# Two feed-forward matrix products as pairs of 64-partition matmuls in the column halves of the array

## The chip, the cores and the metric

The kernel runs on one core of a Trainium2 chip. The metric is the device time in microseconds of one execution, the median of several runs. A core has a matrix engine (TensorE, PE in the profile), a vector engine (VectorE, DVE), a scalar engine (ScalarE, ACT), a general engine (GpSimd, POOL) and an engine that issues transfers (SyncE, SP). Each of them works through its own instructions in the order of the program and waits for the others at semaphores.

## What is computed

Attention over 8 batches, 8 heads, 576 positions and 64 features, in which only the 32 largest scores of each row take part, and behind it a feed-forward block with the activation h·cos(h). All of it is in fp32.

```python
scores = scale * np.matmul(q, k.transpose(0, 1, 3, 2))          # scale = 1/8
kth = np.partition(scores, -top_k, axis=-1)[..., -top_k:-top_k + 1]   # top_k = 32
scores = np.where(scores >= kth, scores, -1000000000.0)
attn = np.exp(scores - np.max(scores, axis=-1, keepdims=True))
attn = attn / (np.sum(attn, axis=-1, keepdims=True) + 1e-09)
attn_out = np.matmul(attn, v)
x = attn_out.transpose(0, 2, 1, 3).reshape(4608, 512)            # (B*S, H*D)
h = x @ w_in                                                     # 512 -> 2048
g = h * np.cos(h)
out = g @ w_out                                                  # 2048 -> 512
```

## The kernel before

**Units and slots.** The 4608 token rows are cut into 36 blocks of 128. A unit is one block and one pair of heads, so there are 144 units, four to a block. The main loop (`slot`, L753) runs once for each unit. In a slot the program issues: VectorE's search for the 32 largest scores of unit i; ScalarE's mask and exponentials of unit i-1; the splitting of unit i-2 into half words by GpSimd and two transfers that bring it back transposed (`send`, L738); TensorE's scores of coming units; once in four slots P@V of four units (`values`, L456); and pieces of the feed-forward work of earlier blocks (`feed`, L671, by the table `plan`, L746). The order on each engine is fixed when the program is built; nothing is decided while it runs.

**Scores** (`scores`, L235). Contraction over 64 features, 64 query rows at a time: a matmul occupies 64 rows and 64 columns of the array, and the two heads and the two row halves of a unit take the four quarters. Each has 448 key columns, and a second group has the last 128 (into the bank called `rim`). A score buffer (`sc`, two of them) is free again when VectorE has read it at L267 (`fold_high`).

**P@V** (`values`, L456). The contraction runs over keys, in four chunks of 128 and one of 64 (`v_tail`, shared between heads). The output is transposed: 64 features of a head are the output partitions and 128 tokens the moving columns. The two heads of a pair go to the two column halves of the array, in alternating order: 128 rows by 64 columns for `v`, 64 by 64 for `v_tail`. The result lies in the free part of the `rim` banks. ScalarE's copy of the score ends (L257) reads the same banks, and VectorE multiplies by the reciprocal sums and writes `xT` (L491, L499).

**FF1** (`ff1`, L537). For a block, 16 slices f of 128 hidden features, each the sum over four chunks of 128 input features: the stationary operand is a 128 by 128 slice of `w_in`, the moving one is `xT`, 128 features by 128 tokens. One call makes two slices (8 matmuls), two calls fill one PSUM bank `mm` of 512 columns, so 16 matmuls are what stands together in the trace. ScalarE empties the bank twice (L567, L569 in `take_first`); GpSimd and ScalarE then make the cosine and the product g.

**FF2** (`ff2`, L618). For a block, 16 matmuls accumulate one 128 by 512 output `o`: the stationary operand is a 128 by 128 slice of g, the moving one 512 columns of `w_out`. One call makes two of the 16, two calls stand together. ScalarE scales the result into `ob` and sends it off (L638, L640). `mm` and `o` share two PSUM banks.

**Order on TensorE in the steady part.** One block, that is four slots: scores of two units, P@V of four units, FF2, FF1, FF2, FF1, scores of two units, FF2, FF1, FF2, FF1. After the last unit the program drains (`drain`, L823): two more P@V calls, each of two units, and the rest of the feed-forward work.

An fp32 matmul appears in the trace as two passes, each with a weight load (PEld) and a matmul row (PE). So the 2304 matmuls of FF1 are 4608 rows and the 576 of FF2 are 1152.

Of the kernel before, what the change touches and what calls it, by code (L numbers as in the profile page):

```python
# [17 lines left out]
P = 128  # L18
# [12 lines left out]
def kernel(  # L31
# [9 lines left out]
    nc = tc.nc  # L41
    ctx.enter_context(tc.manual_schedule())
    B, H, D, S = qT.shape
# [5 lines left out]
    NF = DF // P  # L49
# [29 lines left out]
    NC = DM // P  # L79
    FC = CW // P  # L80
    w_in = []
    w_out = []
    chunks = []
    for i in range(DF // CW):
        w = consts.tile([P, NC, CW], F32, tag=f"w_in{i}", name=f"w_in{i}")
# [4 lines left out]
    w = consts.tile([P, NF, DM], F32, tag="w_out", name="w_out")  # L90
# [421 lines left out]
    for w in widths:  # L512
        blk = {"t0": t0, "w": w, "left": 0, "g": [], "gated": []}
# [17 lines left out]
    def open_bank():  # L531

        if ff["open"] + len(full) == 2:
            take_banks()
        ff["open"] += 1

    def ff1(blk, i):  # L537
        w = blk["w"]
        nf = 256 // w
        part = i % 4  # L540
        if part == 0:
            blk["g"].append(ffw.tile([P, 1024], F32, tag="g", name="g", bufs=CHUNKS))
            blk["x"] = ffw.tile([P, 1024], F32, tag="x", name="x", bufs=XB)
            ff["live"] += 1
        if part % 2 == 0:
            open_bank()
            blk["mm"] = ps.tile([P, 512], F32, tag="mm", name="mm", bufs=2)
        g, mm = blk["g"][-1], blk["mm"]
        for a in range(nf):
            f = i * nf + a  # L550
            at = (part % 2 * nf + a) * w
            for c in range(NC):
                nc.tensor.matmul(  # L553
                    mm[:, at : at + w],
                    w_in[f // FC][:, c, (f % FC) * P : (f % FC + 1) * P],
                    blk["xT"][:, c],
                    start=c == 0,
                    stop=c == NC - 1,
                )
        if part % 2 == 0:  # L560
            return
        ff["open"] -= 1
        full.append((take_first, blk, g, blk["x"], mm, part // 2))
# [54 lines left out]
    def ff2(blk, i, f0):  # L618
        w = blk["w"]
        if f0 == 0:  # L620
            open_bank()
            blk["o"] = ps.tile([P, 512], F32, tag="mm", name="o2", bufs=2)
        o = blk["o"]
        per = 1024 // w
        for f in range(f0, f0 + 2):
            g = blk["g"][f // per]
            at = (f % per) * w + i * P
            nc.tensor.matmul(  # L628
                o, g[:, at : at + P], w_out[f], start=f == 0, stop=f == NF - 1
            )  # L630
        if f0 + 2 < NF:
            return
        ff["open"] -= 1
        full.append((take_second, blk, i, o))
# [27 lines left out]
    def item(kind):  # L662
        if not (can_first, can_second)[kind]():
            return False
        if kind == 0:
            ff1(*first.popleft())
        else:
            ff2(*second.popleft())
        return True
# [181 lines left out]
    for i in range(NU):  # L851
        ff["now"] += 1
        wq["ready"] = wq["done"]
        u, w, x = (units[i - n] if n <= i else None for n in range(3))
# [46 lines left out]
```

## Time and profile before

| | |
|---|---|
| median of 3 runs | 1413.0 us (1412.85 to 1414.05) |
| span of the profiled execution | 1410.6 us |
| TensorE busy | 1354.6 us (96%) |
| weight loads busy | 977.2 us (69%) |
| VectorE busy | 1336.9 us (95%) |
| GpSimd busy | 1165.3 us (83%) |
| ScalarE busy | 1140.9 us (81%) |
| granted clock of TensorE, mean | 0.975 |

The span goes from the first to the last instruction of one execution; the median of the runs is over whole executions. In the rows below, times are microseconds from the start of the span. A timeline row has start, length, engine, line and operation, the tiles written and read, the part of the array (rows*columns) for TensorE, the shape of the moving operand and the number of instructions merged (x32); what stands in brackets is how long the engine was idle before it and who ended that. The length of a merged row runs from the first start to the last end, and consecutive matmuls overlap in it, since the start of one does not wait for the end of the one before. The chain of waits follows the end of the execution back, at each step to what released it. The ends of matmuls are modelled in such a trace, so steps from start to start are used for TensorE.

### The profile page before, as it was taken

Reading aid. Unit: us, or ns where it says so; the run is one execution under the profiler, and the core shown is the slowest. Engines: PE = TensorE matmul, PEld = TensorE weight load, DVE = VectorE, ACT = ScalarE, POOL = GpSimd, SP = SyncE. Lnnn points to the kernel's source line nnn. Section 1 sums busy time; section 2 is a strip of 40 time slices with the busy share of each in tenths; the row PEclk is TensorE's granted clock in tenths of the full one; section 3 lists DMA queues with packets and bytes.
Section 4 is the critical chain, followed back from the end, with each engine's and each line's share of the span. In section 5 each row is a group of like instructions: output and inputs, shape, how many; then the busy total and the mean of one; then the engine's idle time right before and its main releaser. Section 6 shows DMA issues by size and latency. Waiting matters only on the chain.

```text
span 1410.6 us, 32284 instructions
## 1 busy us (share of the span) xinstructions
PE 1354.6 (96%) x11264; PEld 977.2 (69%) x11264; DVE 1336.9 (95%) x5004; ACT 1140.9 (81%) x2043; POOL 1165.3 (83%) x804
## 2 busy tenths in 40 slices
PE   5558999999999999999999999999999999999998
PEld 3445777777777777777777777777777777777775
DVE  7999999999999999999999999999999999999931
ACT  7887888888888888888888888888888888888831
POOL 4778988888888888888888888888888888898810
PEclk6788999999999999999999999999999999999999
DMA  9566776867675576668666576666766566655540
GB/s 291 193 196 181 204 178 169 203 172 196 162 177 152 161 199 159 181 160 197 174 170 159 152 181 187 170 170 160 207 165 165 158 174 166 148 157 146 152 101 15
DMA packets 427442, 240.12 MB, mean 170 GB/s; under 512 B 375952, under 2 KB 392592, under 8 KB 427280
## 3 DMA queue, kind: packets, MB, share of 16 engines
q1 hardware_dynamic: 420720, 224.22, 61.3%
q10 hardware_dynamic: 6560, 13.85, 2.8%
q8 instruction: 88, 1.44, 0.4%
q14 instruction: 74, 0.61, 0.1%
HBM read 45.09 MB, written 101.19 MB: 104 GB/s over the span
## 4 chain that ended last, share of the span: by engine, by line
PE 91%; DVE 7%; ACT 1%; DMA 0%; POOL 0%; issue 0%; SPq 0%; POOLq 0%
PE o L628 36%; PE mm L553 35%; PE rim L475 10%; PE sc L242 8%; DVE top L359 3%; PE rim L242 2%; DVE rest L364 2%; DVE low L364 1%; DVE rest L267 1%; DVE w_out L151 0%; DVE w_in L151 0%; DMA st<-in_moe_w_in_dram 0%; PE warm L844 0%; DVE low L275 0%; ACT s L387 0%; ACT s L378 0%
## 5 line engine op out<-in xcount | busy, mean ns | idle before, releaser
L553 PEld LDWEIGHTS mm<-xT,w_in 128*128 128x128 f32 x4608 | 537.9, 192 | 70.4 <-issue 65.5
L553 PE MATMUL mm<-xT,w_in 128*128 128x128 f32 x4608 | 539.2, 275 | 2.4 <-DVE xT L491 1.7
L628 PE MATMUL o<-w_out,g 128*128 128x512 f32 x1152 | 524.7, 599 | 0.0
L359 DVE MAX8 top<-rest 128x8 f32<-128x288 f32 x1152 | 479.0, 451 | 0.0
L364 DVE MATCH_REPLACE8 rest<-top,rest 128x288 f32<-128x288 f32 x864 | 376.7, 444 | 0.0
L628 PEld LDWEIGHTS o<-w_out,g 128*128 128x128 f32 x1152 | 207.7, 190 | 219.5 <-issue 214.8
L410 POOL COPY halves<-s 128x2304 uint16<-128x2304 uint16 x140 | 294.9, 2107 | 43.3 <-ACT s L387 40.1
L378 ACT ACTIVATE s<-s,top 128x576 f32<-128x576 f32 x288 | 207.6, 768 | 111.1 <-DVE top L352 99.0
L359 DVE MAX8 top<-low 128x8 f32<-128x288 f32 x576 | 241.8, 449 | 0.4 <-POOL low L292 0.4
L387 ACT ACTIVATE s<-s,nd 128x576 f32<-128x576 f32 x288 | 220.4, 769 | 1.1
L292 POOL TENSOR_TENSOR low<-low,rest 128x576 int32<-128x576 int32 x141 | 199.3, 1413 | 11.0
L283 POOL TENSOR_TENSOR low<-s 128x576 int32<-128x576 int32 x141 | 199.6, 1415 | 6.4 <-ACT s L259 6.4
L598 POOL TENSOR_TENSOR x<-g,x 128x1024 f32<-128x1024 f32 x68 | 161.2, 2370 | 5.7
L242 PE MATMUL sc<-k,q 64*64 64x448 f32 (+1 forms) x1120 | 145.6, 564 | 16.2 <-DVE low L275 9.8
L615 POOL TENSOR_TENSOR g<-g,x 128x1024 f32<-128x1024 f32 x68 | 161.0, 2367 | 0.0
L257 ACT COPY s<-rim 64x256 f32<-64x256 f32 (+1 forms) x280 | 103.1, 368 | 61.6 <-PE rim L475 60.0
L475 PE MATMUL rim<-ring,v 128*64 128x128 f32 (+1 forms) x2560 | 139.0, 268 | 0.0
L475 PEld LDWEIGHTS rim<-ring,v 128*64 128x64 f32 x2560 | 130.0, 139 | 6.5 <-issue 5.7
L253 ACT COPY s<-sc 128x896 f32<-128x896 f32 (+1 forms) x144 | 128.4, 892 | 3.3 <-PE sc L242 3.2
L567 ACT ACTIVATE g<-mm 128x512 f32<-128x512 f32 x144 | 85.2, 592 | 56.5 <-PE mm L553 55.5
L364 DVE MATCH_REPLACE8 low<-top,low 128x288 f32<-128x288 f32 x288 | 125.4, 443 | 0.0
L267 DVE TENSOR_TENSOR rest<-sc,s 128x576 f32<-128x576 f32 x144 | 107.7, 748 | 7.1 <-ACT s L259 6.6
(55 smaller groups left out, 1155.7 us busy)
## 6 DMA issues: line engine op xcount, KB each, us to landing
rows<-halves SPq DMA_DIRECT2D x140, 640.0 KB, 3.5
out_dram<-ob ACTq DMA_DIRECT2D x36, 256.0 KB, 2.1
q<-in_q_dram SPq DMA_DIRECT2D x31, 288.0 KB, 4.4
st<-in_moe_w_in_dram SPq DMA_DIRECT2D x16, 512.0 KB, 5.8
v<-in_v_dram SPq DMA_DIRECT2D x32, 256.0 KB, 4.2
k<-in_k_dram SPq DMA_DIRECT2D x31, 144.0 KB, 4.2
k<-in_k_dram SPq DMA_DIRECT2D x32, 128.0 KB, 4.5
st<-in_moe_w_out_dram SPq DMA_DIRECT2D x8, 512.0 KB, 5.1
```

Of the source, the lines that this page charges most:

```text
L242: nc.tensor.matmul(to[r0 : r0 + rows, rim_bank(r0, j) if k0 else place(u["hp"], j), 0 : k1 - k0], st["q"][d, q0 : q0 + rows], st["k"][d, k ...
L283: nc.gpsimd.tensor_tensor(out=u["low"].bitcast(I32), in0=s[:, :, 0:HS], in1=s[:, :, HS:S], op=ALU.add)
L292: nc.gpsimd.tensor_tensor(out=low, in0=low, in1=u["rest"][:, :, HS:S].bitcast(I32), op=ALU.subtract)
L359: nc.vector.max(to[:, j], src[:, j])
L364: nc.vector.match_replace(rest[:, j], to[:, j], src[:, j], NEG)
L378: nc.scalar.activation(out=s[:, j], in_=s[:, j], func=AF.Prelu, bias=less[:, j], scale=1.0, alpha=FAR)
L387: nc.scalar.activation(out=s[:, j], in_=s[:, j], func=AF.Exp, bias=nd[:, j : j + 1], scale=SCALE, accum_out=den[:, j, 0:1],)
L410: nc.gpsimd.tensor_copy(out=halves[:, :, 0 : 2 * S], in_=s.rearrange("p (k h) -> p h k", h=2))
L475: nc.tensor.matmul(to[d, r], lhsT, rhs, start=(bank, j) not in begun, stop=c == NT - 1 and u in us[-2:] and r0 + rows == P,)
L553: nc.tensor.matmul(mm[:, at : at + w], w_in[f // FC][:, c, (f % FC) * P : (f % FC + 1) * P], blk["xT"][:, c], start=c == 0, stop=c == NC - 1,)
L598: nc.gpsimd.tensor_tensor(out=x, in0=g, in1=x, op=ALU.subtract)
L628: nc.tensor.matmul(o, g[:, at : at + P], w_out[f], start=f == 0, stop=f == NF - 1)
```

## The change

Both products issue two matmuls where there was one. The stationary operand is cut into columns 0 to 63 and 64 to 127 (D is 64, P is 128), and the two outputs go to partitions 0 to 63 and 64 to 127 of the same PSUM region; the moving operand is the same for both. The two halves alternate within the accumulation. Nothing else is touched: the other engines' instructions, the order of the groups on TensorE and the waits between engines stand as before.

```diff
@@ ff1
             for c in range(NC):
-                nc.tensor.matmul(
-                    mm[:, at : at + w],
-                    w_in[f // FC][:, c, (f % FC) * P : (f % FC + 1) * P],
-                    blk["xT"][:, c],
-                    start=c == 0,
-                    stop=c == NC - 1,
-                )
+                for r0 in range(0, P, D):
+                    nc.tensor.matmul(
+                        mm[r0 : r0 + D, at : at + w],
+                        w_in[f // FC][:, c, (f % FC) * P + r0 : (f % FC) * P + r0 + D],
+                        blk["xT"][:, c],
+                        start=c == 0,
+                        stop=c == NC - 1,
+                    )
@@ ff2
             at = (f % per) * w + i * P
-            nc.tensor.matmul(
-                o, g[:, at : at + P], w_out[f], start=f == 0, stop=f == NF - 1
-            )
+            for r0 in range(0, P, D):
+                nc.tensor.matmul(
+                    o[r0 : r0 + D], g[:, at + r0 : at + r0 + D], w_out[f], start=f == 0, stop=f == NF - 1
+                )
```

## Prediction

> **What bounds the kernel now.** First the page: where the engines are full, and what the chain that ended last is made of.
>
> ```profile
> span 1410.6 us, 32284 instructions
> ...
> PE   5558999999999999999999999999999999999998
> ...
> DVE  7999999999999999999999999999999999999931
> ...
> PE 91%; DVE 7%; ACT 1%; DMA 0%; POOL 0%; issue 0%; SPq 0%; POOLq 0%
> ```
>
> TensorE and VectorE are both at nine tenths or more from the fourth slice to the last two, so the page alone does not say which of them sets the pace. The chain does: 91% of it is TensorE. I then looked at the chain inside the steady part, around one block of 128 tokens, which the program works on in four slots (columns: start, length, piece).
>
> ```profile
> 303.68 3.63 PE o L628 x8
> 307.31 3.57 PE mm L553 x32
> 310.88 3.44 PE o L628 x8
> 314.31 3.57 PE mm L553 x32
> ...
> 340.37 3.63 PE o L628 x8
> ```
>
> The piece at 303.68 comes back at 340.37: a block takes 36.69 us, and the chain through it is TensorE's work alone. An fp32 matmul is recorded as two passes, so x32 is 16 matmuls of FF1 (the first product, L553) and x8 is four of FF2 (the second, L628). Next, how much room VectorE has in the steady part, and what it waits for there.
>
> ```profile
> core 0: us, PE busy (x) PEld busy (x) DVE busy (x) ACT busy (x) POOL busy (x), PEclk, DMA share, GB/s
> 113.00:1340.00 1227.00, 1226.35 (x10466) 887.49 (x10460) 1215.45 (x4601) 1027.61 (x1833) 1080.60 (x736) 1.00 0.66 171
> ```
>
> ```profile
> DVE xT L491 <- ACT s L257: 7.1, 24, 0.8
> DVE xT L499 <- ACT s L257: 3.9, 7, 1.5
> ```
>
> In these 1227 us (33.4 blocks) TensorE is idle for 0.65 us and VectorE for 11.55 us, 0.35 us a block. Of that 11.0 us is one wait, that of the xT multiply for ScalarE's copy at L257. Two timeline rows of one block show who is late behind ScalarE:
>
> ```profile
> 303.72 0.74 ACT L257 COPY s<-rim 64x256 f32<-64x256 f32 x2 [1.64 <-PE rim L475]
> 304.50 0.49 DVE L499 TENSOR_TENSOR xT<-rim,ring 128x128 f32<-128x128 f32 x2 [0.30 <-ACT s L257]
> ```
>
> ScalarE stood 1.64 us until P@V (L475) was done with the PSUM banks they share, and VectorE stood 0.30 us behind it. So TensorE sets the pace and VectorE follows 1% behind it: **whatever TensorE saves beyond 0.35 us a block will not be seen in the time.** From here everything is worked out per block.
>
> **The change part by part.** It adds no arithmetic and no other engine's instruction: each matmul of 128 output partitions becomes two of 64, written to the two halves of the same PSUM region, in the alternating order of P@V. 5760 passes become 11520, and as many weight loads, each of 64 columns instead of 128.
>
> *FF1, 128 passes a block.* The shape after the change (128 rows, 64 columns, 128 moving) is that of P@V.
>
> ```profile
> 718.52 0.39 PE L553 MATMUL mm<-xT,w_in 128*128 128x128 f32 x2
> 721.87 0.28 PE L553 MATMUL mm<-xT,w_in 128*128 128x128 f32 x1
> 704.38 0.39 PE L475 MATMUL rim<-ring,v 128*64 128x128 f32 x4
> 707.66 0.28 PE L475 MATMUL rim<-ring,v 128*64 128x128 f32 x2
> ```
>
> The first pair of rows are the 2nd and the 32nd pass of one FF1 group: 30 steps in 3.35 us, 0.1117 us each. The second pair are the 2nd and the 32nd pair of passes of one P@V: 30 steps in 3.28 us, 0.1093 us for two halves together (x2 within 0.28 us, the length of one: they do run at once). The saving is 0.0023 us a pass, 0.30 us a block; two decimals of the rows leave it between 0.22 and 0.38.
>
> *FF2, 32 passes a block.* No row shows a half of 128 rows with 512 moving columns. The nearest are the scores, 64 rows and 448 columns.
>
> ```profile
> 708.40 0.59 PE L628 MATMUL o<-w_out,g 128*128 128x512 f32 x1
> 710.55 0.59 PE L628 MATMUL o<-w_out,g 128*128 128x512 f32 x1
> 703.08 0.56 PE L242 MATMUL sc<-k,q 64*64 64x448 f32 x4
> 703.46 0.29 PE L242 MATMUL rim<-k,q 64*64 64x128 f32 x4
> ```
>
> FF2 now steps 0.43 us (five steps from 708.40 to 710.55). Four score passes, two of them in either column half and with the same moving operand, start together and the next set follows 0.38 us later: 0.85 ns a column, against 0.84 for FF2. So a pair should also take 0.43 us, and I take no change. The bounds: the 0.0023 us that P@V gains over FF1 (a gain of 0.07 us a block), and 0.05 us a pass if a pair stalled as the first one of P@V does (next rows; a loss of 1.6 us a block). I stay at the near end because the P@V pairs and the 448-column sets both stream without such a stall.
>
> *Switches of the tiling mode, two a block, P@V to FF2 and scores to FF2.*
>
> ```profile
> 707.87 0.70 PE L628 MATMUL o<-w_out,g 128*128 128x512 f32 x1
> 723.96 0.29 PE L242 MATMUL rim<-k,q 64*64 64x128 f32 x4
> 724.18 0.70 PE L628 MATMUL o<-w_out,g 128*128 128x512 f32 x1
> 724.71 0.59 PE L628 MATMUL o<-w_out,g 128*128 128x512 f32 x1
> 704.00 0.29 PE L475 MATMUL rim<-ring,v_tail 64*64 64x128 f32 x4
> 704.22 0.33 PE L475 MATMUL rim<-ring,v 128*64 128x128 f32 x2
> ```
>
> After P@V's last pair (707.66) FF2 starts 0.21 us later and its second pass another 0.53 us later: 0.74. In one mode it would be 0.11 and 0.43: **0.20 us saved**. After the scores it is 0.22 and 0.53 (723.96, 724.18, 724.71); that switch stays, but into the mode of P@V, as from v_tail to v: 0.22 and then 0.16 instead of 0.11 for the first pair (704.00, 704.22, 704.38), 0.05 more than a step where FF2 now pays 0.10. **0.05 us saved.** From FF1 into the scores there is a switch before and after; no row shows it out of the column mode at this size, and I leave it as it is, with the 0.05 between the two kinds of first step as the bound on either side, twice a block.
>
> *Sum for TensorE:* 0.30 + 0.20 + 0.05 = 0.55 us a block, 18.4 us over 33.4 blocks, more than the 11.0 us that VectorE waits. So VectorE becomes the bound, if TensorE can get far enough ahead of it. The two nearest waits of TensorE in the block:
>
> ```profile
> 296.24 0.75 DVE L267 TENSOR_TENSOR rest<-sc,s 128x576 f32<-128x576 f32 x1
> 298.44 0.93 PE L242 MATMUL sc<-k,q 64*64 64x448 f32 x8
> 312.16 0.68 ACT L569 ACTIVATE x<-mm,quarter 128x512 int32<-128x512 f32 x1
> 314.15 1.05 PE L553 MATMUL mm<-xT,w_in 128*128 128x128 f32 x8
> ```
>
> The second score group needs the buffer that L267 reads: it starts 1.45 us after L267 ends. FF1 needs the bank that L569 empties: 1.31 us. So TensorE can lead by about 1.3 us more than now, and 0.30 to 0.8 us is enough for xT to find its operands ready. What is late next is then TensorE itself, behind VectorE at the scores, where it stands at no cost. **Steady part: 11.0 us** of the 11.55.
>
> *The end.* In the last two slices of the page VectorE has little left (3 and 1 tenths) and TensorE is full: there the time is TensorE's.
>
> ```profile
> 1342.40:1411.00 68.60, 26.14 (x224) 25.92 (x223) 0.99 0.19 55
> ```
>
> Seven FF1 groups, 224 passes by 0.0023, are 0.5 us, and the two P@V calls of the drain, each followed by FF2, are 0.4: **0.9 us**. And TensorE enters the end with the lead it has won, at most 1.3 us, of which I take **1.0**.
>
> *The instructions.* Twice as many FF1 and FF2 instructions have to be fetched, by a queue of their own:
>
> ```profile
> q8 instruction: 88, 1.44, 0.4%
> ```
>
> Even if all its 88 packets were doubled, that is 0.8% of the transfer engines' time. P@V already runs through two loads and two matmuls in 0.11 us, the rate that FF1 now gets, so I cost it at nothing; if a fetch came late, TensorE's lead of 1.3 us would cover it in the steady part, and it would show whole only in the end.
>
> *Sum:* 11.0 + 0.9 + 1.0 = 12.9 us off the span of 1410.6, 1397.7. The median of the runs, 1413.0, lies 2.4 us above this span, so the forecast is **1400 us**.
>
> **The rivals.**
>
> *A: FF2's pairs are a little dearer, and TensorE keeps the pace.* At 0.01 us a pass more, a block saves 0.55 - 0.32 = 0.23 us, 7.7 us over the steady part: 1405. For it: no row has such a pair at 512 columns. Against it: 0.85 and 0.84 ns a column.
>
> *B: slower. The next weight load is not hidden in FF2's pairs.* Place: every FF2 pass; price: the 0.05 us by which P@V's first pair, whose load nothing covers, exceeds a step. 1152 passes by 0.05 are 57.6 us, less 36 blocks by 0.55, 19.8: 1451. It decides from 0.017 us a pass on, where 32 passes eat the 0.55. For it: no row shows a load behind such a pair; against it: P@V hides the same loads beside passes a quarter as long.
>
> *C: it does not do what it is for, since VectorE is the bound already* and its 0.35 us a block is a fixed round trip. Then only the end is left: 1412. Against it: VectorE's wait stands behind P@V, which would come earlier.
>
> *D: VectorE does not bind* because its 99% has waits inside the records: all 36 blocks save 0.55 us, 1393. Against it: the two rows of waits account for 11.0 of its 11.55 idle.
>
> *E: no load is hidden between halves of the same rows.* Both products would then step as P@V's first pair does, 0.16 us: 4608 passes by 0.048 and 1152 by 0.05 are 279 us, less 0.25 by 36 for the switches: 1683. The P@V rows, 0.1093 us with 128 rows in both halves, speak against it. [...]
>
> **How the numbers follow.** The forecast gets 0.70, A 0.11, B 0.11, C 0.04, D 0.03, E 0.01. What a measurement here can tell from no change is about 0.2%, 2.8 us: faster are the forecast, A and D (0.84), the same is C (0.04), slower B and E (0.12). The range runs from 1396, which lets VectorE win its whole 11.55, the full lead of 1.3, 0.9 at the end and some 3 us of waits too short to show as idle, to 1409, which is A with half its saving left: it holds the forecast and A, 0.81.
>
> **What would show it.** In the profile after: FF1 groups of 64 passes in about 3.5 us with pairs 0.109 apart; FF2 pairs 0.43 apart; 0.11 between P@V's last pair and FF2; a block of 36.35 instead of 36.69 us; VectorE's waits at xT nearly gone and new waits of TensorE for VectorE (L267) or ScalarE, some 0.2 us a block; a chain with far more VectorE in it. The forecast is wrong if FF2 pairs step over 0.45 us, if pairs start one after the other, or if the xT wait stays while TensorE's blocks get shorter.

## The result, and the profile after

| | before | after |
|---|---|---|
| median of the runs | 1412.9 us | 1400.5 us |
| span of the profiled execution | 1410.6 us | 1397.0 us |

The ratio is 0.991, with a 95% interval of 0.9896 to 0.9924 (four runs of each; the 1413.0 us above are the median of three). The page of the changed kernel:

```profile
span 1397.0 us, 43804 instructions
## 1 busy us (share of the span) xinstructions
PE 1339.6 (96%) x17024; PEld 905.7 (65%) x17024; DVE 1334.2 (96%) x5004; ACT 1140.6 (82%) x2043; POOL 1169.3 (84%) x804
...
PE 59%; DVE 35%; ACT 2%; DMA 2%; POOL 1%; issue 1%; SPq 0%; DVEq 0%; POOLq 0%; ACTq 0%
```

TensorE and VectorE are busy for as large a share as before, so the busy shares tell nothing. The chain does: VectorE's part went from 7% to 35%, TensorE's from 91% to 59%. The windows view of the steady part (same columns as in the prediction) and VectorE's waits in it (who waits, for whom: us in total, times, longest):

```profile
113.00:1330.00 1217.00, 1214.45 (x15798) 821.79 (x15793) 1214.56 (x4606) 1028.78 (x1836) 1086.54 (x737) 1.00 0.66 174
```

```profile
DVE xT L499 <- ACT s L257: 1.2, 1, 1.2
DVE xT L491 <- ACT s L257: 0.7, 1, 0.7
DVE rest L267 <- ACT s L257: 0.6, 1, 0.6
```

VectorE was idle for 11.55 us in the 1227 us of the steady part and is now idle for 2.44 in 1217, in three waits. The 31 waits at xT have become two. Then TensorE's timeline, at the turn from P@V to FF2 and FF1 (L553 and L628 of before are L554 and L630 here):

```profile
337.59 0.39 PE L475 MATMUL rim<-ring,v 128*64 128x128 f32 x4
337.81 0.60 PE L630 MATMUL o<-w_out,g 128*64 128x512 f32 x2
339.96 1.03 PE L630 MATMUL o<-w_out,g 128*64 128x512 f32 x4
341.25 0.49 PE L554 MATMUL mm<-xT,w_in 128*64 128x128 f32 x5
344.52 0.39 PE L554 MATMUL mm<-xT,w_in 128*64 128x128 f32 x4
```

Two FF2 passes lie within 0.60 us, the length of one: the halves do run at once. Five pairs lie between 337.81 and 339.96, 0.43 us each, as full matmuls had taken. FF1's first and 31st pairs start at 341.25 and 344.52: 30 steps of 0.109 us. And FF2 starts 0.22 us after the last but one pair of P@V, that is 0.11 us after the last: the switch is gone.

What TensorE waits for now is what the prediction named, the score buffer that VectorE's L267 reads:

```profile
404.36 0.75 DVE L267 TENSOR_TENSOR rest<-sc,s 128x576 f32<-128x576 f32 x1
405.16 0.21 PEld L242 LDWEIGHTS sc<-k,q 64*64 64x64 f32 x8 [0.19 <-DVE rest L267]
405.16 0.61 PE L242 MATMUL sc<-k,q 64*64 64x448 f32 x4
```

The second score group starts 0.05 us after L267 ends, where it started 1.45 us after it before the change. It is so in 15 of the 32 blocks between 150 and 1280 us; in the others the distance is 0.2 to 0.9 us. Waits as short as this hardly show as idle time of TensorE, whose matmul ends are modelled.

### The profile page after: what moved, and what is told of

Same layout as the page of the kernel before. It is cut to its first block, busy times and chain, and to the rows that moved or that the text cites. A ratio compares the mean times of both kernels' runs of the same rounds, so it can differ in the third digit from the quotient of the medians.

```text
span 1397.0 us, 43804 instructions
## 1 busy us (share of the span) xinstructions
PE 1339.6 (96%) x17024; PEld 905.7 (65%) x17024; DVE 1334.2 (96%) x5004; ACT 1140.6 (82%) x2043; POOL 1169.3 (84%) x804
## 4 chain that ended last, share of the span: by engine, by line
PE 59%; DVE 35%; ACT 2%; DMA 2%; POOL 1%; issue 1%; SPq 0%; DVEq 0%; POOLq 0%; ACTq 0%
PE o L630 23%; PE mm L554 23%; DVE top L359 16%; DVE rest L364 10%; PE rim L475 7%; PE sc L242 5%; DVE low L364 3%; DVE rest L267 3%; PE rim L242 1%; DMA ring<-rows 1%; DMA rows<-halves 1%; DVE xT L491 0%; DVE top L347 0%; DVE w_out L151 0%; DVE top L352 0%
## 5 line engine op out<-in xcount | busy, mean ns | idle before, releaser
L554 PEld LDWEIGHTS mm<-xT,w_in 128*64 128x64 f32 x9216 | 512.8, 137 | 85.1 <-issue 57.2
L554 PE MATMUL mm<-xT,w_in 128*64 128x128 f32 x9216 | 528.7, 273 | 3.2 <-DVE xT L491 2.1
L630 PE MATMUL o<-w_out,g 128*64 128x512 f32 x2304 | 520.0, 594 | 0.0
L630 PEld LDWEIGHTS o<-w_out,g 128*64 128x64 f32 x2304 | 158.6, 137 | 254.1 <-issue 253.1
L242 PE MATMUL sc<-k,q 64*64 64x448 f32 (+1 forms) x1120 | 146.9, 568 | 16.9 <-DVE low L275 10.2
L267 DVE TENSOR_TENSOR rest<-sc,s 128x576 f32<-128x576 f32 x144 | 107.7, 748 | 7.0 <-ACT s L259 6.4
```

The lines of the kernel that those rows point to most:

```text
L242: nc.tensor.matmul(to[r0 : r0 + rows, rim_bank(r0, j) if k0 else place(u["hp"], j), 0 : k1 - k0], st["q"][d, q0 : q0 + rows], st["k"][d, k ...
L554: nc.tensor.matmul(mm[r0 : r0 + D, at : at + w], w_in[f // FC][:, c, (f % FC) * P + r0 : (f % FC) * P + r0 + D], blk["xT"][:, c], start=c ...
L630: nc.tensor.matmul(o[r0 : r0 + D], g[:, at + r0 : at + r0 + D], w_out[f], start=f == 0, stop=f == NF - 1)
```

## The experiments

### One product alone in pairs

`e1_ff1_only` has the changed `ff1` and the `ff2` of before; `e2_ff2_only` the other way round.

```diff
 e1, ff1:
+                for r0 in range(0, P, D):
+                    nc.tensor.matmul(mm[r0 : r0 + D, at : at + w], ...)
 e1, ff2:
             nc.tensor.matmul(o, g[:, at : at + P], w_out[f], ...)

 e2, ff1:
                 nc.tensor.matmul(mm[:, at : at + w], ...)
 e2, ff2:
+            for r0 in range(0, P, D):
+                nc.tensor.matmul(o[r0 : r0 + D], g[:, at + r0 : at + r0 + D], w_out[f], ...)
```

> Only FF1 in pairs, FF2 as before. Theory (TensorE sets the pace until VectorE binds; FF1's pairs step 0.0023 us faster, every change of the tiling mode costs 0.15 to 0.20 us): a block now has six more changes between FF1 and FF2. FF2 to FF1, four a block, by the nearest change of before (FF1 to scores: 0.10 late and a first step 0.04 longer), 0.14 each; FF1 to FF2, two a block, like P@V to FF2, 0.20 each; together 0.97, less FF1's 0.30: a block of 37.36 instead of 36.69 us, 36 blocks by 0.67 = 24 us slower than before, about 1437 us. Rival 1 (the gain of the change is FF1's pace, changes of mode cost nothing between FF1 and FF2): faster than before by the 11 us that VectorE has to give, about 1402 us.

> Only FF2 in pairs, FF1 as before. Theory: P@V to FF2 and scores to FF2 save 0.20 and 0.05 a block; new are FF2 to FF1, four a block, by 0.20 (column mode to full mode, as P@V to FF2 before), and FF1 to FF2, two a block, by 0.14; FF2's pace is the same. 1.08 less 0.25 is 0.83 us a block more than 36.69: 37.5 us, 30 us slower than before, about 1443 us. Rival 2 (the gain is FF2's alone, from the saved change after P@V): faster than before by 0.25 a block, about 1404 us.

Measured, one run each: 1442.3 us and 1441.4 us, beside 1412.0 of the kernel before. Both halves of the change, each by itself, are 2% slower than no change. The chain of e1 (TensorE's alone in this stretch), around one block:

```profile
536.64 3.63 PE o L629 x8
540.27 3.65 PE mm L554 x64
543.91 3.63 PE o L629 x8
547.54 3.65 PE mm L554 x64
```

and the chain of e2:

```profile
532.35 3.43 PE o L629 x16
535.78 3.77 PE mm L553 x32
539.55 3.58 PE o L629 x16
543.13 3.77 PE mm L553 x32
```

Every FF2 of e1 takes 3.63 us, where before only those after P@V and after the scores did, and FF1 takes 3.65 instead of 3.57, its faster pace eaten by the entry. In e2 FF1 takes 3.77, 0.20 more, and FF2 after FF1 3.58 instead of 3.44; only FF2 after P@V is quick, 3.43. So a change of mode cost 0.14 to 0.20 us here, whichever way it went, and rivals 1 and 2 fall: the gain needs both products in one mode. e1 came out 5 us above its expectation, though its steady blocks were as expected: from one L267 to the one four slots on it is 37.38 us where 37.36 was worked out. What is over lies in the start: slots 8 to 11 took 47.6 us, where before they took 42.3. In three runs of this study, `e1`, `e4` and `e5`, the granted clock was at half for 17 to 20 us from about 100 us on, and these four slots took 46.3 to 47.6 us; in the nine others it was at half for 13.7 us there, and the slots took 41.8 to 43.3. Which of the two brings the other about was not tested.

### Is VectorE the floor?

`e6` and `e7` take one small instruction from VectorE, and leave the result as it is, before and after the change:

```diff
     def sums(u):
-        den = small.tile([P, 2], F32, tag="den", name="den")
-        nc.vector.tensor_reduce(out=den, in_=u["den"], axis=mybir.AxisListType.X, op=ALU.add)
-        u["den"] = den
+        u["den"] = u["den"][:, :, 0]
```

> The kernel before without VectorE's small sum that adds 1e-9 to the row sums ahead of the reciprocal (a row sum is at least 1, since the largest score contributes exp(0), and in fp32 1 + 1e-9 is 1). It costs VectorE 0.06 us a slot, by the steps from MAX8 to MAX8 with and without it. Theory: TensorE sets the pace, so nothing but the first slots changes, under 1 us: 1412 to 1413 us. Rival 5 (VectorE is the bound): 144 by 0.06 = 8.6 us less.

> The changed kernel without the same small sum. Theory: VectorE binds at 36.36 us a block and drops to 36.12, TensorE's own work is 36.14, so a block gains about 0.2 us: 33 by 0.2 = 7 us, about 1393.5 us. Rival 3 (VectorE is not what binds after the change): 1400 us as before the edit.

Measured: before the change 1412.0 us, a ratio of 1.0 to the kernel before (0.9991 to 1.0009): nothing, so rival 5 falls. After the change 1393.7 us, a ratio of 0.987 (0.9856 to 0.9883), against 0.991 (0.9896 to 0.9924) of the changed kernel, so rival 3 falls. The same 0.06 us a slot is worth nothing in one kernel and 5 to 7 us in the other (its median is 1400.5 us, and 1398.9 when it ran once more, below). That is the plainest sign of which engine sets the pace. The blocks say the same: from one L267 to the one four slots on, the median is 36.70 us before and in `e6`, 36.37 after the change, and 36.14 in `e7`, which is TensorE's own work. The chain of `e7` from 200 to 1300 us is TensorE's alone again (L552 is FF1 there, L628 FF2, L473 P@V and L242 the scores):

```profile
by line: PE mm L552 38.5%; PE o L628 38.5%; PE rim L473 11.3%; PE sc L242 9.2%; PE rim L242 2.4%
```

`e7` is also the fastest version of this study, faster than both kernels.

`e4` and `e5` take more from VectorE, before and after the change:

```diff
-            search(top[:, :, 1 + 8 * k : 9 + 8 * k, 1], low, low, more, () if more else between)
+            search(top[:, :, 1 + 8 * k : 9 + 8 * k, 1], low, low, False, () if more else between)
```

> The kernel before, with one of VectorE's replacing passes over the low halves left out in every slot (its two MATCH_REPLACE8 and their value loads, 0.86 us a slot; the last eight values found are then those found before them). Theory (TensorE sets the pace of the steady part before the change): the block stays at 36.69 us, and only the first dozen slots, where VectorE is busy all the time and no FF work runs, are 0.86 us shorter each: about 10 us, 1403 us. Rival 5 (VectorE already was the bound before): 144 slots by 0.86 = up to 120 us less.

> The changed kernel with the same VectorE work left out. Theory: VectorE is no floor any more, and the whole saving of TensorE, 0.55 us a block, shows: a block of 36.14 us, and a difference to the kernel before with the same work left out of 36 by 0.55 = 20 us, against 12.4 with all of VectorE's work: about 1383 us. Rival 6 (TensorE saved no more than the 12 us that were seen, and VectorE hides nothing): the difference between the two stays at about 12 us.

Measured: 1409.6 us (ratio 0.9991, 0.9977 to 1.0004; rival 5 falls again) and 1395.4 us (0.9881, 0.9868 to 0.9895). The chain of e4 through one block:

```profile
521.65 4.08 PE rim L475 x80
525.74 3.63 PE o L628 x8
529.37 3.57 PE mm L553 x32
532.94 3.44 PE o L628 x8
536.37 3.57 PE mm L553 x32
542.04 3.63 PE o L628 x8
```

and the chain of e5:

```profile
516.30 4.08 PE rim L475 x80
520.38 3.43 PE o L630 x16
523.81 3.49 PE mm L554 x64
527.30 3.43 PE o L630 x16
530.74 3.49 PE mm L554 x64
536.33 3.58 PE o L630 x16
```

Here both are TensorE's chains, and they can be set side by side: P@V 4.08 and 4.08; FF2 after P@V 3.63 and 3.43; FF1 3.57 and 3.49; FF2 after the scores 3.63 and 3.58. With four FF1 groups a block that is 0.20 + 0.32 + 0.05 = 0.57 us, where the prediction had 0.20 + 0.30 + 0.05. So TensorE did save all of it, and in the changed kernel the part above VectorE's slack does not show: a block goes from 36.70 to 36.37 us there, and from 36.70 to 36.14 between e4 and e5 (medians from L267 to L267).

The two totals were expected wrongly. The 10 us that the start was to gain did not come, in either kernel. In e4, VectorE's saving there turned into waits for the banks that P@V, the scores and xT share, over the stretch from 60 to 135 us:

```profile
ACT s L257 <- PE rim L475: 12.3, 2, 8.9
...
DVE xT L499 <- ACT s L257: 7.0, 1, 7.0
...
DVE xT L491 <- ACT s L257: 4.3, 1, 4.3
```

In the kernel before, the first two of these are 7.7 and 1.5 us there, and the third is none. And the difference between the two medians is 14.2 us, not 20; the ten runs of e4 lie between 1408.0 and 1417.4 us, so its median is a rough one. The blocks decide against rival 6, the medians alone would not have.

### Less work for TensorE

`e3` leaves one chunk of four out of FF1 in the changed kernel:

```diff
-            for c in range(NC):
+            for c in range(NC - 1):
...
-                        stop=c == NC - 1,
+                        stop=c == NC - 2,
```

> The changed kernel with FF1 summed over three of its four chunks of input features (the fourth is left out). TensorE has 32 pairs of passes by 0.109 us = 3.5 us a block less to do. Theory (VectorE binds the steady part after the change): the block stays at 36.3 to 36.4 us, and only the end is shorter, seven FF1 groups by 8 pairs by 0.109 = 6 us, and up to 2 us of lead: 1392 to 1395 us. Rival 3 (TensorE still sets the pace): 36 blocks by 3.5 us less, 126 us, until another engine binds; anything below 1380 us speaks for it.

Measured: 1409.4 us in a single run, beside 1412.0 of the kernel before. So it is slower than the changed kernel with all its work. It was expected 6 to 8 us faster; rival 3 (below 1380) is further off. Two stretches in the windows view of e3 (columns: length; busy time of PE, PEld, DVE, ACT, POOL; the granted clock; DMA) show what neither theory had:

```profile
481.10:484.50 3.40, 3.40 (x46) 3.07 (x40) 3.40 (x14) 3.40 (x9) 2.90 (x3) 0.50 0.38 139
484.50:500.00 15.50, 15.50 (x190) 10.22 (x190) 14.93 (x58) 11.35 (x19) 13.04 (x9) 1.00 0.65 171
```

```profile
478.43 0.45 PE L242 MATMUL rim<-k,q 64*64 64x128 f32 x8 [0.62 <-ACT s L257]
480.10 0.98 PE L242 MATMUL sc<-k,q 64*64 64x448 f32 x8 [1.22 <-DVE rest L267]
480.90 0.46 PE L242 MATMUL rim<-k,q 64*64 64x128 f32 x8
481.12 1.09 PE L475 MATMUL rim<-ring,v_tail 64*64 64x128 f32 x16
482.14 4.86 PE L475 MATMUL rim<-ring,v 128*64 128x128 f32 x64
```

TensorE first waits for VectorE's L267, as the theory has it, 1.22 us at a time. After such gaps its clock was granted at 0.50 for 3.4 us, and the P@V that falls into that stretch takes 4.86 us instead of 3.71. There are seventeen such stretches in the steady part. Blocks without one mostly take 36.3 to 36.4 us from one L267 to the same one four slots on, as in the changed kernel; blocks with one mostly take 36.9 to 37.1. The last L267 comes at 1334.94 us, 11.9 us later than in the changed kernel, and seventeen blocks of 0.6 to 0.7 us more make 10 to 12. The end, which was to be 6 us shorter, is only 1.3 us shorter; TensorE waits there once for a transfer, for 2.98 us, and its clock goes to half once more.

Which gaps came ahead of the half clock can be read from the same trace. The seventeen stretches start whole multiples of 3.413 us apart, so the trace is read here in windows of that length. TensorE was busy for 0.46 to 0.49 of each window just ahead of one, and for 0.55 or more of every other window of the steady part at full clock:

```profile
477.69:481.10 3.41, 1.56 (x28) 0.76 (x28) 3.41 (x15) 2.13 (x6) 3.19 (x4) 1.00 0.68 216
1139.89:1143.30 3.41, 1.88 (x40) 1.16 (x40) 3.41 (x15) 2.14 (x4) 3.18 (x4) 1.00 0.73 249
```

The first of these is followed by the half clock shown above. The second is the least busy one that was followed by full clock. So in e3 the half clock came after windows in which TensorE was busy for less than half of the time, 0.46 to 0.49. Where between 0.49 and 0.55 the border lies, and what sets it, was not shown.

To part the clock from the floor, `e9` leaves out an eighth as much, and the changed kernel ran beside it once more:

```diff
-            for c in range(NC):
+            nk = NC - 1 if f % 8 == 0 else NC
+            for c in range(nk):
...
-                        stop=c == NC - 1,
+                        stop=c == nk - 1,
```

> The changed kernel with one chunk of four left out in two of FF1's sixteen slices (f = 0 and 8): TensorE has 4 pairs of passes by 0.109 = 0.44 us a block less to do, an eighth of what was left out in e3_three_chunks, which came out at 1409 us with the granted clock at half in some twenty stretches of 3.4 us. Theory (VectorE is the floor, and it was the halved clock after TensorE's idle time that cost more in e3): the block stays at 36.36 us at full clock, the end is under 1 us shorter: 1399 to 1400.5 us. Rival 3 (TensorE sets the pace): 33 by 0.44 = 15 us less, 1386 us. Rival 7 (less work on TensorE is slower for another reason than the clock): an eighth of e3's loss or more, 1401.5 us or above, with the clock at full.

> The changed kernel once more, beside e9_two_slices_less on the same chip: 1400.5 us.

Measured: 1400.3 us (ratio to the kernel before 0.9917, 0.9902 to 0.9932) and 1398.9 us (0.9906, 0.989 to 0.9923). The windows view of the steady part of e9:

```profile
113.00:1330.00 1217.00, 1206.74 (x15519) 805.50 (x15518) 1213.86 (x4603) 1030.35 (x1834) 1086.56 (x737) 1.00 0.68 174
```

The clock is at 1.00, TensorE is idle for 10.3 us where the changed kernel has 2.6, VectorE is as full as there, and the time is the same within the intervals. So TensorE's work is no longer what the time is made of, and rival 3 falls. Rival 7 is not decided by the medians: 1400.3 is below its 1401.5 us, but e9 lies 1.4 us above the changed kernel run beside it, within the intervals and yet as much as an eighth of e3's loss. The blocks speak against it: the median from L267 to L267 is 36.37 us in both, and the last L267 comes at 1323.20 and 1323.51 us. That the clock is what made e3 slow is argued from its blocks; no run changed the clock alone.

### The order of the halves

`e8` exchanges the two loops of FF1, so that four chunks (eight passes) of one half come before those of the other:

```diff
-            for c in range(NC):
-                for r0 in range(0, P, D):
+            for r0 in range(0, P, D):
+                for c in range(NC):
```

> The changed kernel, but in FF1 the two halves do not alternate: all four chunks of the first 64 partitions, then all four of the other 64. Theory (two passes run at once only where neighbours in program order go to different halves): inside a run of eight passes of one half nothing runs beside it except at its borders, so FF1 takes nearly twice as long, 4608 pair steps by up to 0.109 = up to 500 us more: 1750 to 1900 us. Rival 4 (the halves have queues of their own and order does not matter): about 1400 us, as the changed kernel.

Measured: 1481.6 us in a single run, so neither theory. TensorE's timeline at the start of one FF1 group:

```profile
510.13 0.38 PE L554 MATMUL mm<-xT,w_in 128*64 128x128 f32 x2
510.24 0.55 PE L554 MATMUL mm<-xT,w_in 128*64 128x128 f32 x4
510.46 0.49 PE L554 MATMUL mm<-xT,w_in 128*64 128x128 f32 x5
```

The group begins at 510.02 with single passes, 0.11 us apart, and from 510.46 on, at the fifth, two start together. The rows do not name the half; by the program the first eight passes are of one half, so the second of these two is taken to be the first pass of the other half, ahead of its turn. At the end of the group the line shows such a change of order:

```profile
513.92 0.64 PE L630 MATMUL o<-w_out,g 128*64 128x512 f32 x1
514.02 0.49 PE L554 MATMUL mm<-xT,w_in 128*64 128x128 f32 x3
```

A pass of FF2 (L630) starts 0.10 us ahead of three passes of FF1 (L554) that stand before it in the program. So TensorE, unlike what the opening section says of every engine, did not start its passes strictly in the order of the program here. By the pairing above the first pass of the other half started together with the fifth of a run of eight, ahead of the three behind that one; why at the fifth was not shown. From 510.46 on eight passes take 0.49 us instead of 0.44. In sum a block takes 38.70 us where TensorE needs 36.14 in e5. The alternating order of the change saved TensorE these 2.6 us a block.

## Why the prediction was right, point by point

*What bounds.* TensorE before, by 1%: shown by e6 and e4, where less work for VectorE leaves the block at 36.70 us.

*FF1's pace, 0.30 us a block.* 0.109 us a pair, as the P@V rows had it; 0.32 by the chains of e4 and e5.

*FF2's pace, no change.* 0.43 us a pair at 512 columns, which no row had shown; eight pairs take 3.43 us in e5, where eight full passes took 3.44. So the loss of 0.05 a pass is out, and with it rival B, and rival A, which had 0.08 us more in eight pairs.

*Switches, 0.25 us a block.* 0.20 and 0.05 in e5. The switch from FF1 to the scores, which was left as it is, stayed: before the scores FF1 takes the 3.57 and 3.49 us that it takes before FF2, in the chains of e4 and e5 (TensorE's starts put the switch at 0.09 us before and 0.10 after). What the prediction did not say is how much hangs on changing both products: e1 and e2 turn the gain of 12 us into a loss of 30.

*VectorE becomes the floor.* The steady part was to give 11.0 us. From the last L267, which moved from 1335.18 to 1323.06, it gave 12.1:

```profile
1335.18 0.75 DVE L267 TENSOR_TENSOR rest<-sc,s 128x576 f32<-128x576 f32 x1
...
1342.47 0.27 PE L553 MATMUL mm<-xT,w_in 128*128 128x128 f32 x1
```

```profile
1323.06 0.75 DVE L267 TENSOR_TENSOR rest<-sc,s 128x576 f32<-128x576 f32 x1
...
1329.67 0.33 PE L554 MATMUL mm<-xT,w_in 128*64 128x128 f32 x2
```

(the first two rows are of before, the other two of after). The idle time fell by 9.1 us, and VectorE's busy time by 2.7, 1336.9 to 1334.2, with the same 5004 instructions. Its records overlap by some 0.08 us (the L267 row of before ends at 1335.93, and the next row starts at 1335.85), so a shorter wait would not show as idle but as busy time, which would account for the 2.7; the prediction had put such waits into its range and not into its sum.

*The lead, 1.0 us.* The first of the seven FF1 groups of the end starts 7.29 us after the last L267 before and 6.61 after: 0.7. It starts 0.06 us after L570 (L569 of before) ends, where it was 0.74 us before. So TensorE already waits there for the nearer of the two waits that were named, and no more lead was to be had.

*The end, 0.9 us.* From that FF1 to the end of the span it was 68.1 us and is 67.3: 0.8.

*The instructions, nothing.* Their queue moved 133 packets instead of 88, 0.7% of the transfer engines' time, and FF1 kept P@V's pace.

So 12.1 + 0.7 + 0.8 = 13.6 us of span, against 12.9; the medians differ by 12.4. The mechanism held in each part; that the forecast is within 1 us of the median is luck in part, since the steady part gave 1.1 us more than its term, and the median after lies 3.5 us above the span, where 2.4 had been added. Rival C falls with e6, where less work for VectorE saved nothing, and rival D with e7, where it did, and with e5 (the saving that VectorE hid is there once VectorE is out of the way). Rival E falls with FF1's 0.109 us a pair, in which two loads, recorded at 137 ns each on average, are started as well: here the loads were hidden beside matmuls on the same 128 rows. How, no row tells.

## What to carry to other kernels

Where two engines are both full, find the one that follows, add up how long it waits per round, and cap every saving of the other near that (here 11.0 us were counted and 12.1 came); an edit of a few hundredths of a microsecond on either engine, tried with and without the change, then tells which of them sets the pace. A change between full-width matmuls and column halves cost TensorE 0.14 to 0.20 us in e1 and e2, so put all neighbours into one mode or none, and alternate the halves matmul by matmul (a block took 38.70 us in e8, where they do not alternate, and 36.14 in e7, where they do). Once TensorE is the one that was freed and stands idle in gaps like the 0.62 and 1.22 us of e3, look at its granted clock, 0.50 for 3.4 us there, before counting on more savings.

## What the runs showed of the hardware that was not expected

- A quarter less of FF1's work made the kernel 9 us slower than the changed one, with the granted clock at 0.50 in stretches of 3.4 us. They followed windows of 3.41 us in which TensorE was busy for 0.46 to 0.49; after the other windows at full clock, of 0.55 and more, the clock stayed at full.
- In e8 passes of TensorE did not start in the order of the program: a pass of FF2 started 0.10 us ahead of three of FF1, and by the pairing a pass of the other column half started with the fifth of a run of eight, ahead of the three behind it.
- Changing the mode cost 0.14 to 0.20 us in e1 and e2 also between full-width fp32 matmuls and column halves of the same shape, in either direction.
